# A planned one-core kernel (gated linear attention, then a two-layer MLP): a planner that follows both DMA streams in time, the first attention blocks in the first layer's PSUM banks, and decay factors taken straight from PSUM

## The chip, the cores and the metric

One core of one Trainium2 chip. The metric is the device time of one execution in microseconds, as the median of three runs; the profile shows one more execution, with its own time.

## The reference

```python
def _attn_ref(q, k, v, f_logit):            # (4, 8, 768, 48) each
    f = 1.0 / (1.0 + np.exp(-f_logit))
    for t in range(S):
        state = f[:, :, t, :, None] * state + np.einsum('bhd,bhe->bhde', k[:, :, t], v[:, :, t])
        y[:, :, t] = np.einsum('bhd,bhde->bhe', q[:, :, t], state)

def _moe_ref(x, w_in, w_out):               # x (3072, 384), w_in (384, 2048), w_out (2048, 384)
    h = x @ w_in
    g = 0.5 * (h + np.sqrt(h * h + 4.0))
    return g @ w_out
```

The tokens of all heads of a batch are laid side by side, so that the output of the attention is the input of the MLP.

## The kernel before, in words

The 3072 tokens are 24 blocks of 128 (six to a batch, so that the state starts anew at blocks 0, 6, 12 and 18), and two blocks are a **pair**, p = 0 to 11. A pair goes through these steps:

- **Loads.** SP issues eight DMAs per pair (f, q, k, v for two blocks, 192 KB each, in runs of 192 bytes). The weights, eight pieces of `w_in` and eight of `w_out`, are issued on POOL and cast to fp16 on the way.
- **Logs** (`add_logs`): ScalarE takes exp and log of f into `ls`; POOL or VectorE splits `ls` into two fp16 parts, `lhi` and `llo`.
- **Decays** (`add_decays`): TensorE sums the logs down the block into a bank `hps`, in whose last columns two half-block sums per head stand as well. ScalarE makes `ea` and `eap` of it by exp; POOL or VectorE multiplies them into q and k (`qk`); v is cast to fp16; VectorE copies the half-block sums to `nls`. In `add_gammas` VectorE adds neighbouring sums into `gi`, ScalarE takes the exp, and VectorE spreads it over `gam`, the decay of the state from block to block.
- **Attention** of a block (`add_attention`, `add_state`): transposes of `qk` (on TensorE for pairs 0 to 4, by DMA for 5 to 11), scores `sc`, masked `pm`, the state update `u` and `sn`, the output `y`, its transpose into `xT`.
- **First layer** (`add_mlp1`): four steps per pair. A step is 12 matmuls into two banks `hps`, two squares `hsq` and one root `r` on ScalarE, two gates `g` on VectorE, which free the banks. There are five banks `hps` (NH), which the decays use too, two banks "a" (NA) for the attention, and one bank `o` (NO).
- **Second layer** (`add_mlp2`): per block 16 matmuls into `o` in four quarters; quarter n needs gates of step n and pieces 2n and 2n+1 of `w_out`; then a copy to `o_sb` and a store, issued by POOL or SP.

ScalarE needs one table for exp and log and another for the root, so the logs and decays are gathered in seven stretches (`GROUPS`): in stretch g the decays of group g and the logs of group g+1.

The order is not written by hand. A `Plan` takes every step with a duration, what it waits for and which buffers it takes; it simulates the engines and, among steps that can start at about the same time, takes the one with the lowest due time. The due times are the tables `BASE` (by part and pair) and `SHIFT` (by kind of step), and `ENG` says which engine takes a step that two could take. What comes out is one fixed order on each engine, in which every engine runs in order. Loads had one queue, in the order of `ORDER`, and a pass over both streams (`flows`) gave the DMAs their landing times for the next pass.

Of the kernel before, what the change touches and what calls it, by code (L numbers as in the profile page):

```python
# [63 lines left out]

class Op:
    __slots__ = ("eng", "dur", "deps", "emit", "due", "allocs", "uses", "end", "kind", "dma", "ins", "flow", "issued")

    def __init__(self, eng, dur, emit, deps=(), due=0.0, allocs=(), uses=(), kind=None, dma=None, ins=()):
# [22 lines left out]
class Plan:  # L91
# [39 lines left out]
    def flows(self):  # L131


        todo = {"SP": [], "POOL": []}
        for op in self.order:
            if not isinstance(op, str) and op.dma is not None:
                todo[op.eng].append([op.issued, op.dma[0], op])
        t = 0.0
        while todo["SP"] or todo["POOL"]:
            live = {e: q[0] for e, q in todo.items() if q and q[0][0] <= t + 1e-9}  # L140
            later = [q[0][0] for e, q in todo.items() if q and e not in live]
            if not live:
                t = min(later)
                continue
            rate = {"SP": 0.35, "POOL": 0.65} if len(live) == 2 else {e: 1.0 for e in live}
            step = min([x[1] / rate[e] for e, x in live.items()] + [a - t for a in later])
            t += step
            for e, x in live.items():
                x[1] -= step * rate[e]
                if x[1] <= 1e-9:  # L150
                    x[2].flow = t + x[2].dma[1] - x[2].issued
                    todo[e].pop(0)

    def run(self, passes=3):
        for n in range(passes):
            for ops in self.queues.values():
                for op in ops:
                    op.end = None
                    for b in op.uses + op.allocs:
                        b.ring.bufs = []  # L160
# [723 lines left out]
```

## Time and profile before

| | before |
|---|---|
| median of 3 runs | 222.13 us (222.03 to 222.53) |
| profiled execution | 222.69 us, of which the span of the trace is 220.9 us |
| busy in the span | TensorE 183.0, ScalarE 170.3, VectorE 156.7, POOL 86.0 us |
| DMA | 32.09 MB, 61.8% of the 16 engines' span on SP's queue, 13.2% on POOL's |

What lies outside of the span is 1.8 us. The ends of TensorE's matmuls are modelled, so that neighbours overlap: its busy time is more than the time that it takes from one start to the next.

### The profile page before, as it was taken

What the parts mean: (1) busy time and instruction counts of PE and PEld (TensorE: products, weight loads), DVE (VectorE), ACT (ScalarE), POOL (GpSimd) and SP (SyncE); (2) the same over time, 40 slices, a digit from 0 to 9 for tenths busy, and PEclk for the clock granted to TensorE, in tenths of its full rate; (3) what the DMA queues carried; (4) which work ended last, traced back from release to release, by engine and by line L of the source; (5) the groups of instructions that cost most, each with busy time, mean ns of one, the idle gap of its engine ahead of it and who ended that gap; (6) DMA issues with size and microseconds to landing.
All of it is one profiled execution on the core that took longest, in us unless ns stands there. A gap on an engine that the chain in (4) does not pass through costs nothing.

```text
span 220.9 us, 4812 instructions
## 1 busy us (share of the span) xinstructions
PE 183.0 (83%) x1870; PEld 132.6 (60%) x1870; DVE 156.7 (71%) x285; ACT 170.3 (77%) x262; POOL 86.0 (39%) x95
## 2 busy tenths in 40 slices
PE   0445837928999999789988998799999999999973
PEld 0223624715777576567666776476677777777641
DVE  5056716836976989998998988998879888663220
ACT  5306339469899999779999999599979999986710
POOL 8959379531014408440993118703900000000010
PEclk9999987995999999999999999999999999999998
DMA  7999999999999999499999999741572302111101
GB/s 135 164 178 168 196 182 201 220 179 214 215 200 239 227 213 187 110 221 154 233 177 184 171 223 186 136 106 53 81 153 47 74 18 58 53 39 37 71 36 71
DMA packets 128262, 32.09 MB, mean 145 GB/s; under 512 B 121088, under 2 KB 127616, under 8 KB 128240
## 3 DMA queue, kind: packets, MB, share of 16 engines
q1 hardware_dynamic: 122032, 26.09, 61.8%
q0 software_dynamic: 6208, 5.70, 13.2%
q8 instruction: 14, 0.23, 0.4%
q14 instruction: 8, 0.07, 0.1%
HBM read 25.17 MB, written 4.72 MB: 135 GB/s over the span
## 4 chain that ended last, share of the span: by engine, by line
PE 54%; ACT 12%; DVE 11%; DMA 10%; SPq 8%; issue 3%; POOL 1%; ACTq 0%; DVEq 0%; POOLq 0%
PE o L788 23%; PE hps L748 21%; SPq L371 8%; DMA ld_v<-in_v_dram 5%; DMA ld_f<-in_f_logit_dram 4%; DVE qk L495 3%; ACT r L763 3%; PE sc L626 2%; ACT hsq L754 2%; DVE gam L555 2%; PE tr L601 1%; ACT ls L438 1%; ACT L851 1%; PE y L649 1%; DMA xT<-y 1%
## 5 line engine op out<-in xcount | busy, mean ns | idle before, releaser
L788 PE MATMUL o<-w_out,g 128*128 128x384 f16 x384 | 73.2, 326 | 2.9 <-DVE o_sb L799 1.4
L771 DVE SCALAR_TENSOR_TENSOR g<-hps,r 128x512 f16<-128x512 f32 x96 | 61.7, 685 | 18.9 <-ACT r L763 18.1
L748 PE MATMUL hps<-xT,w_in 128*128 128x256 f16 x576 | 73.6, 279 | 1.1 <-DMA xT<-y 0.8
L748 PEld LDWEIGHTS <-w_in 128*128 128x128 f16 x576 | 56.1, 100 | 12.9 <-DMA xT<-y 1.2
L754 ACT ACTIVATE hsq<-hps 128x512 f16<-128x512 f32 x96 | 54.5, 592 | 6.9 <-PE hps L748 5.4
L763 ACT ACTIVATE r<-hsq 128x1024 f16<-128x1024 f16 x48 | 50.7, 1057 | 1.4
L788 PEld LDWEIGHTS <-g 128*128 128x128 f16 x384 | 35.3, 97 | 22.6 <-issue 4.0
L803 POOL DMA_DIRECT2D out_dram<-o_sb x13 | 7.3, 563 | 72.4 <-DVE o_sb L799 41.4
L633 DVE TENSOR_TENSOR pm<-sc,mask 128x512 f16<-128x512 f32 x48 | 31.0, 682 | 4.6 <-PE sc L626 4.6
L433 ACT ACTIVATE ld_f<-ld_f 128x768 f32<-128x768 f32 (+1 forms) x14 | 10.7, 763 | 18.2 <-DMA ld_f<-in_f_logit_dram 18.2
L495 POOL TENSOR_TENSOR qk<-ld_q,ea 128x768 f16<-128x768 f32 (+1 forms) x10 | 14.8, 1483 | 19.0 <-ACT ea L489 16.6
L502 POOL CAST v<-ld_v 128x768 f16<-128x768 f32 (+1 forms) x11 | 8.6, 779 | 27.7 <-DMA ld_v<-in_v_dram 27.7
L444 POOL TENSOR_TENSOR llo<-ls,lhi 128x768 f16<-128x768 f32 (+1 forms) x12 | 17.3, 1449 | 3.4 <-DVE lhi L441 2.8
L626 PE MATMUL sc<-qkT 48*128 48x128 f16 x192 | 11.3, 230 | 6.7 <-ACT qkT L605 3.3
L495 POOL TENSOR_TENSOR qk<-ld_k,eap 128x768 f16<-128x768 f32 (+1 forms) x10 | 15.2, 1518 | 0.0
L601 PE MATMUL tr<-ident,qk 128*128 128x128 f16 x80 | 8.7, 267 | 7.7 <-POOL qk L495 5.7
L489 ACT ACTIVATE ea<-hps 128x384 f32<-128x384 f32 x24 | 10.8, 502 | 5.5 <-PE hps L482 5.4
L475 PE MATMUL hps<-lhi,wcent 128*128 128x384 f16 x24 | 8.5, 352 | 7.5 <-POOL lhi L441 7.5
L626 PEld LDWEIGHTS <-qkT 48*128 48x128 f16 x192 | 6.3, 99 | 12.9 <-issue 7.8
L649 PEld LDWEIGHTS <-pm 128*128 128x128 f16 x192 | 10.2, 99 | 4.0 <-issue 2.6
L797 ACT COPY o_sb<-o 128x384 f32<-128x384 f32 x10 | 4.8, 477 | 9.6 <-PE o L788 9.6
L601 PEld LDWEIGHTS <-qk 128*128 128x128 f16 x80 | 6.5, 118 | 9.4 <-POOL qk L495 6.8
(56 smaller groups left out, 237.7 us busy)
## 6 DMA issues: line engine op xcount, KB each, us to landing
ld_f<-in_f_logit_dram SPq DMA_DIRECT2D x24, 192.0 KB, 4.1
ld_q<-in_q_dram SPq DMA_DIRECT2D x24, 192.0 KB, 4.0
ld_k<-in_k_dram SPq DMA_DIRECT2D x24, 192.0 KB, 4.0
ld_v<-in_v_dram SPq DMA_DIRECT2D x24, 192.0 KB, 4.6
out_dram<-o_sb POOLq DMA_DIRECT2D x13, 192.0 KB, 3.3
out_dram<-o_sb SPq DMA_DIRECT2D x11, 192.0 KB, 2.1
w_in<-in_moe_w_in_dram POOLq DMA_DIRECT2D x8, 192.0 KB, 7.0
w_out<-in_moe_w_out_dram POOLq DMA_DIRECT2D x8, 192.0 KB, 5.9
```

The source lines that it names most:

```text
L371: (nc.gpsimd if cast else nc.sync).dma_start(out=T["v16" if cast else name, p][:, r], in_=src_of[name][b][:, c * C:(c + 1) * C, :].rearran ...
L444: eng_of[lg[p, x].eng].tensor_tensor(out=llo[p % NL][:, x:y, :, 0:D], in0=T["ls", p][:, x:y], in1=lhi[p % NL][:, x:y, :, 0:D], op=ALU.subt ...
L495: eng_of[mu[p, x, i].eng].tensor_tensor(out=qk[p % NB][:, x:y, i, :, 0:D], in0=T[name, p][:, x:y], in1=T[e, p][:, x:y], op=ALU.mult)
L601: nc.tensor.transpose(out=tr[:, s * NP + j, :], in_=qk[p % NB][:, i, s, 2 * j:2 * j + 2, :], identity=ident16)
L626: nc.tensor.matmul(out=T["sc", r, s][:, j, :], lhsT=qkT[o:o + D, NP + j, :], rhs=qkT[o:o + D, j, :], start=True, stop=True)
L633: nc.vector.tensor_tensor(out=T["pm", r][:, s], in0=T["sc", r, s], in1=mask16.unsqueeze(1).broadcast_to([128, NP, C]), op=ALU.mult)
L649: nc.tensor.matmul(out=y[:, j, s], lhsT=T["pm", r][:, s, j, :], rhs=T["v16", p][:, i, 2 * j + s, :], start=(c == 0), stop=(c == 0 or s == 1))
L748: nc.tensor.matmul(out=hb[:, a, :], lhsT=w_in16[j2][:, j, a * 128:(a + 1) * 128], rhs=T["xT", p][:, j, :], start=(j == 0), stop=(j == NJ - 1))
L754: nc.scalar.activation(out=T["hsq", p, j4][:, a], in_=T["h", p, j2], func=AF.Square, scale=1.0)
L763: nc.scalar.activation(out=T["r16", p, j4], in_=T["hsq", p, j4], func=AF.Sqrt, scale=0.25, bias=1.0)
L771: nc.vector.scalar_tensor_tensor(out=T["g", p][:, jn:jn + 2, :].rearrange("p a t -> p (a t)"), in0=T["h", p, 2 * j4 + a], scalar=0.5, in1= ...
L788: nc.tensor.matmul(out=T["o", p, i], lhsT=T["g", p][:, jn, i * C:(i + 1) * C], rhs=w_out16[jn // 2][:, jn % 2, :], start=(jn == 0), stop=( ...
```

## The change

- **The planner** carries both DMA streams along with the engines, in time order (`transfer`): a DMA lands when its stream has moved it, with SP at 0.4 and POOL at 0.65 of the rate while both have work. It lets SP issue only while there is room in its queue (`room`), keeps VectorE's `hi`, `lo`, `qk`, `v16` and `wcast` and POOL's work apart in time, and has new durations.
- **Loads** of f, q, k and v have queues of their own with due times (`"L"` in `BASE`), so that their order is free. Pair 2 is loaded and multiplied by the block, too (`FINE`).
- **Weights.** The first piece of each matrix is loaded on SP as fp32 (`wst`) and cast on VectorE. The other 14 still go by POOL, but now behind the v cast of pair 2 (`AFTER`), and in the plan no more than four are under way (`OUTSTANDING`).
- **q and k** of `qk` have engines of their own, and the product of k does not wait for that of q.
- **Banks.** The attention of blocks 0 to 3 takes banks of `hps` instead of the two banks "a" (`EARLY`).
- **Decay factors.** VectorE copies one half-block sum to `nls` and adds the other from PSUM into `gi`; ScalarE's exp writes `gam` itself, in two halves of 64 partitions. The rest of `gam` is set to zero once. The two VectorE steps of `add_gammas` are gone.
- All tables have new numbers.

```diff
-XBAR = [5, 6, 7, 8, 9, 10, 11]
+XBAR = [5, 6, 7, 8, 9, 10, 11, 13, 14, 15, 16, 17, 18, 19, 21, 22, 23, 24, 25, 26, 27]
...
-FINE = [0, 1]
+FINE = [0, 1, 2]
+
+AFTER = {'in': 2, 'out': 2}
+
+OUTSTANDING = 4
...
+EARLY = 4
...
+    RATE = {"SP": 0.4, "POOL": 0.65}
+    ROOM = 2048
...
+    def transfer(self, streams, t, until):
+
+        while t < until - 1e-9:
+            live = [e for e, q in streams.items() if q and q[0][0] <= t + 1e-9]
+            later = [q[0][0] for e, q in streams.items() if q and e not in live]
+            rate = {e: self.RATE[e] if len(live) == 2 else 1.0 for e in live}
+            step = min([streams[e][0][1] / rate[e] for e in live] + [x - t for x in later] + [until - t])
             t += step
...
+                            if eng == "SP" and op.dma is not None:
+                                t = max(t, self.room(op))
+                            elif eng == "POOL":
+                                t = max(t, locked)
+                            elif eng == "DVE" and op.kin in self.PORT:
+                                t = max(t, free.get("POOL", 0.0))
...
+        w_ready[which, i] = []
+        n = i + (8 if which == "out" else 0)
+        for inline in (NPAIR + n in XBAR,):
+            if inline:
+                def direct():
+                    nc.gpsimd.dma_start(out=dst, in_=src)
+
+                op = P.add("p" + which, "POOL", 0.75, direct, due=1.0 * i, dma=(1.3, 384))
+                direct_ops.append(op)
...
-                    nc.vector.tensor_copy(out=nls[b % 2][:, c + r], in_=nl)
+                    if c + r < NC - 1:
+                        nc.vector.tensor_copy(out=nls[b % 2][:, c + r], in_=nl[:, :, 1])
+                    if c + r > 0:
+                        nc.vector.tensor_tensor(out=gi[b % 2][:, c + r - 1], in0=nl[:, :, 0], in1=nls[b % 2][:, c + r - 1], op=ALU.add)
...
+            def ex(b=b, c0=c0, c1=c1):
+                for s in range(2):
+                    nc.scalar.activation(out=gam[b % 2][64 * s:64 * s + 64, c0:c1, :, s], in_=gi[b % 2][64 * s:64 * s + 64, c0:c1],
+                                         func=AF.Exp, scale=-1.0)
...
+    def bank(r):
+
+        return Buf(ring("h", NH) if r < EARLY else ring("a", NA))
...
+    for a, op in zip(direct_ops, direct_ops[OUTSTANDING:]):
+        op.deps.append(a)
+    for op in direct_ops:
+        if AFTER[op.kin[1:]] is not None:
+            op.deps.append(dec[AFTER[op.kin[1:]], PR - 1][1])
```

What this does to the order shows at three places. First, POOL from its last memset on. Before, four pieces of `w_in` stand ahead of its first `lhi`:

```order
L336 MEMSET qk3_113 128x32x16
L396 DMA w_in16_0_94<-in_moe_w_in_dram 128x3x256
L396 DMA w_in16_1_95<-in_moe_w_in_dram 128x3x256
L396 DMA w_in16_2_96<-in_moe_w_in_dram 128x3x256
L396 DMA w_in16_3_97<-in_moe_w_in_dram 128x3x256
L441 CAST lhi0_114<-ls_152 128x8x48
L444 TENSOR_TENSOR llo0_118<-ls_152,lhi0_114 128x8x48
```

Now the first piece on POOL stands behind the casts of v of pair 2 (`v16_335`), and `w_out` from its third piece on behind the `lhi` of pair 3 (`lhi3`):

```order
L448 CAST lhi2_114<-ls_315 128x8x48
L509 CAST v16_335<-ld_v_283 128x384
L404 DMA w_in16_1_93<-in_moe_w_in_dram 128x3x256
...
L451 TENSOR_TENSOR llo2_118<-ls_315,lhi2_114 128x8x48 x2
...
L404 DMA w_in16_7_99<-in_moe_w_in_dram 128x3x256
L502 TENSOR_TENSOR qk2_110<-ld_k_333,eap_501 128x8x48
L502 TENSOR_TENSOR qk2_110<-ld_q_312,ea_499 128x8x48
L404 DMA w_out16_1_101<-in_moe_w_out_dram 128x2x384
L448 CAST lhi3_115<-ls_533 128x16x48
L404 DMA w_out16_2_102<-in_moe_w_out_dram 128x2x384
```

So eight pieces can be issued before `lhi3`, and the other six wait for it. Second, the first DMAs of SP, before (`ld_f_138` to `ld_v_159` are pair 0, the next four pair 1, `ld_f_313` pair 2):

```order
L371 DMA ld_f_138<-in_f_logit_dram 128x8x48 x2
L371 DMA ld_q_141<-in_q_dram 128x8x48 x2
L371 DMA ld_k_144<-in_k_dram 128x8x48 x2
L371 DMA ld_v_159<-in_v_dram 128x8x48 x2
L371 DMA ld_f_191<-in_f_logit_dram 128x8x48 x2
...
L371 DMA ld_f_313<-in_f_logit_dram 128x8x48 x2
```

and now (`ld_f_142` is pair 0, `ld_f_147` pair 1; the fifth f of SP's order is that of pair 3, behind `ld_k_333` of pair 2):

```order
L413 DMA wst_140<-in_moe_w_out_dram 128x2x384
L376 DMA ld_f_142<-in_f_logit_dram 128x8x48
L413 DMA wst_144<-in_moe_w_in_dram 128x3x256
L376 DMA ld_f_142<-in_f_logit_dram 128x8x48
L376 DMA ld_f_147<-in_f_logit_dram 128x8x48 x2
L376 DMA ld_v_155<-in_v_dram 128x8x48 x2
...
L376 DMA ld_f_254<-in_f_logit_dram 128x8x48 x2
L376 DMA ld_v_283<-in_v_dram 128x8x48 x2
L376 DMA ld_q_312<-in_q_dram 128x8x48 x2
L376 DMA ld_k_333<-in_k_dram 128x8x48 x2
```

The two blocks' loads of pairs 0 and 1 are now grouped by kind, f and v ahead of q and k. Third, ScalarE where the first layer begins. Before, the log of f of pair 2 is followed by two steps of the first layer, and the decays of pair 2 come after them, in a stretch of their own:

```order
L438 ACTIVATE ls_413<-ld_f_313 128x768
L551 ACTIVATE gi_354<-gi_354 128x8
L754 ACTIVATE hsq_437<-hps_392 128x512
L754 ACTIVATE hsq_437<-hps_393 128x512
L851 ACT_TABLE_LOAD
L763 ACTIVATE r16_460<-hsq_437 128x1024
...
L849 ACT_TABLE_LOAD
L489 ACTIVATE ea_546<-hps_510 128x384
```

Now the decays of pair 2 (`ea_499`) and the exp and log of f of pair 3 (`ld_f_374`) stand ahead of the first square:

```order
L660 CAST y16_414<-y_415 128x384
L496 ACTIVATE ea_499<-hps_442 128x384
L496 ACTIVATE eap_501<-hps_442 128x384
...
L440 ACTIVATE ld_f_374<-ld_f_374 128x768
L445 ACTIVATE ls_533<-ld_f_374 128x768
L555 ACTIVATE gam0_120<-gi0_124 64x8 x2
L758 ACTIVATE hsq_560<-hps_535 128x512
```

Seven steps of the first layer then follow with no exps or logs between them; before, the stretch stands behind the first two.

## Rows read from the trace of the kernel before

**Rows 1.** The page's busy line of the core.

```profile
PE 183.0 (83%) x1870; PEld 132.6 (60%) x1870; DVE 156.7 (71%) x285; ACT 170.3 (77%) x262; POOL 86.0 (39%) x95
```

**Rows 2.** Windows: stretch, its length, busy us (instructions) per engine, granted clock, DMA, GB/s.

```profile
0.00:53.50 53.50, 27.46 (x284) 19.46 (x284) 26.20 (x58) 27.45 (x46) 35.63 (x51) 0.93 1.08 182
80.00:160.00 80.00, 73.32 (x846) 53.04 (x845) 72.19 (x129) 72.54 (x117) 40.49 (x31) 1.00 0.84 162
160.00:200.00 40.00, 40.00 (x389) 30.61 (x388) 32.29 (x54) 36.13 (x53) 1.61 (x3) 1.00 0.26 61
```

**Rows 3.** Timeline of ScalarE: start, us, instruction, idle before and what ended it.

```profile
3.59 0.52 ACT L433 ACTIVATE ld_f<-ld_f 128x384 f32<-128x384 f32 x1 [1.57 <-DMA ld_f<-in_f_logit_dram]
16.84 0.52 ACT L433 ACTIVATE ld_f<-ld_f 128x384 f32<-128x384 f32 x1 [5.29 <-DMA ld_f<-in_f_logit_dram]
31.20 0.84 ACT L433 ACTIVATE ld_f<-ld_f 128x768 f32<-128x768 f32 x1 [6.29 <-DMA ld_f<-in_f_logit_dram]
46.05 0.84 ACT L433 ACTIVATE ld_f<-ld_f 128x768 f32<-128x768 f32 x1 [4.62 <-DMA ld_f<-in_f_logit_dram]
48.19 1.09 ACT L754 ACTIVATE hsq<-hps 128x512 f16<-128x512 f32 x2
```

**Rows 4.** Timeline of SP: two issues of f, with nothing but loads between them.

```profile
50.16 1.83 SPq L371 DMA_DIRECT2D ld_f<-in_f_logit_dram  x2
57.61 1.57 SPq L371 DMA_DIRECT2D ld_f<-in_f_logit_dram  x2
```

**Rows 5.** Timeline of POOL: three issues of weights.

```profile
3.72 3.23 POOL L396 DMA_DIRECT2D w_in<-in_moe_w_in_dram  x4
32.02 2.19 POOL L396 DMA_DIRECT2D w_out<-in_moe_w_out_dram  x3
36.71 2.16 POOL L396 DMA_DIRECT2D w_out<-in_moe_w_out_dram  x3
```

**Rows 6.** Timeline of ScalarE: a stretch of exps and logs begins and ends; a root.

```profile
65.08 1.28 ACT L849 ACT_TABLE_LOAD   x1
71.35 1.06 ACT L754 ACTIVATE hsq<-hps 128x512 f16<-128x512 f32 x2
114.94 1.06 ACT L763 ACTIVATE r<-hsq 128x1024 f16<-128x1024 f16 x1
```

**Rows 7.** The chain that ended last: start, us, what.

```profile
70.79 0.89 PE tr L601 x16
...
76.17 1.31 PE hps L748 x12
77.48 0.65 PE o L788 x4
```

**Rows 8.** Groups of VectorE by line: tile, shape, count | busy us, mean ns | idle before.

```profile
L633 DVE TENSOR_TENSOR pm<-sc,mask 128x512 f16<-128x512 f32 x48 | 31.0, 682 | 4.6 <-PE sc L626 4.6
...
L555 DVE TENSOR_TENSOR gam<-gi,half 128x8 f32<-128x8 f32 (+3 forms) x9 | 7.8, 861 | 4.6 <-ACT gi L551 4.6
L495 DVE TENSOR_TENSOR qk<-ld_q,ea 128x768 f16<-128x768 f32 x4 | 6.4, 1612 | 0.1
L546 DVE TENSOR_TENSOR gi<-nls 128x4 f32<-128x4 f32 (+3 forms) x9 | 5.0, 552 | 0.2
L502 DVE CAST v<-ld_v 128x768 f16<-128x768 f32 x3 | 2.5, 838 | 1.7 <-DMA ld_v<-in_v_dram 1.7
```

**Rows 9.** Timelines of VectorE and POOL: gi and qk beside POOL and alone.

```profile
11.78 1.02 DVE L546 TENSOR_TENSOR gi<-nls 128x4 f32<-128x4 f32 x1
11.78 0.99 POOL L495 TENSOR_TENSOR qk<-ld_q,ea 128x384 f16<-128x384 f32 x1
67.28 0.96 DVE L495 TENSOR_TENSOR qk<-ld_q,ea 128x768 f16<-128x768 f32 x1
68.42 0.16 DVE L546 TENSOR_TENSOR gi<-nls 128x4 f32<-128x4 f32 x1
```

**Rows 10.** Timeline of ScalarE: the exp of gi and what it waited for.

```profile
141.52 0.20 ACT L551 ACTIVATE gi<-gi 128x4 f32<-128x4 f32 x1 [2.50 <-DVE gi L546]
```

More of the change, by code (lines that the diff above doesn't have):

```diff
@@ L107, in add @@
         op = Op(eng, dur, emit, due=due, **kw)
+        op.kin = queue
         self.queues.setdefault((eng, queue), []).append(op)
@@ L129, in ready @@
         return t
[L131 to L146, printed above, removed]
+    def transfer(self, streams, t, until):
[4 more added lines that the diff above has]
+            step = min([streams[e][0][1] / rate[e] for e in live] + [x - t for x in later] + [until - t])
@@ L147, in flows @@
             t += step
-            for e, x in live.items():
+            for e in live:
+                x = streams[e][0]
                 x[1] -= step * rate[e]
                 if x[1] <= 1e-9:
[L151 to L160, printed above, removed]
-            self.order = []
-            self.once()
-            if n + 1 < passes:
-                self.flows()
@@ L166, in once, with room, run @@
-    def once(self):
+                    x[2].done = t
+                    x[2].end = t + self.LAG + (self.CROWD if len(live) == 2 else 0.0)
+                    streams[e].pop(0)
+        return until
+    def room(self, op):
+        n = op.dma[1]
+        for x in reversed(self.sent):
+            n += x.dma[1]
+            if n > self.ROOM:
+                return x.done - op.dur
+        return 0.0
+    def run(self):
         heads = {k: 0 for k in self.queues}
         free = dict(START)
-        dma_free = 0.0
-        served = []
+        streams, clock, self.sent, locked = {"SP": [], "POOL": []}, 0.0, [], 0.0
@@ L331 @@
     gam = [konst.tile([128, NC, NP, 2], FP32, name=f"gam{i}") for i in range(2)]
-    nls = [konst.tile([128, NC, NP, 2], FP32, name=f"nls{i}") for i in range(2)]
+    nls = [konst.tile([128, NC, NP], FP32, name=f"nls{i}") for i in range(2)]
+    gi = [konst.tile([128, NC, NP], FP32, name=f"gi{i}") for i in range(2)]
+    for t in gam:
+        nc.vector.memset(t, 0.0)
     for t in lhi + llo:
@@ L613, in add_attention @@
             add_state(r - 1, p, due + 1.0)
-        sc_b = [Buf(ring("a", NA)) for _ in range(2)]
+        sc_b = [bank(r) for _ in range(2)]
         def sc():
@@ L805, in add_mlp2 @@
             oo = oc_op[p, i] = P.add("ev", None, {"DVE": 0.555, "ACT": 0.49}, oc, at=p * PR + i, deps=[last], p=p, due=due, allocs=[os_b], uses=[o_b])
-            st_op[p, i] = P.add("out", None, {"SP": 0.5, "POOL": 0.85}, st, at=p * PR + i, deps=[oo], p=p, due=due, uses=[os_b], dma=(0.6, 1.8))
-    for what in ORDER.split():
-        if what[0] == "P":
-            for n in "fqkv":
-                add_load(int(what[1:]), n)
-        elif what[0] in "io":
-            for i in range(int(what[1]), int(what[2]) + 1):
-                add_weight("in" if what[0] == "i" else "out", i)
-        else:
-            for n in what[:-1]:
-                add_load(int(what[-1]), n)
+            st_op[p, i] = P.add("out", None, {"SP": 0.5, "POOL": 0.6}, st, at=p * PR + i, deps=[oo], p=p, due=due, uses=[os_b], dma=(0.6, 128))
     for p in range(NPAIR):
         for n in "fqkv":
-            if (n, p, 0) not in ld:
-                add_load(p, n)
+            add_load(p, n)
+    for which in ("in", "out"):
+        for i in range(8):
+            add_weight(which, i)
     NG = len(GROUPS)
@@ L839 @@
         add_mlp2(p)
-    if WDMA:
-        for (which, i), op in w_ready.items():
-            if AFTER[which] is not None:
-                op.deps.append(dec[AFTER[which], PR - 1][1])
+    for a, op in zip(direct_ops, direct_ops[OUTSTANDING:]):
[3 more added lines that the diff above has]
+            op.deps.append(dec[AFTER[op.kin[1:]], PR - 1][1])
     P.run()
```

184 lines of the change are left out of this document (80 added, 104 removed), and 15 rows, old and new, of tables (BASE, SHIFT).

## The prediction, as it was put on record before the kernel ran

> **What bounds the kernel now.** I read the page first. TensorE is busy 83% of the span and ScalarE 77% [rows 1], so neither alone explains it. The windows then split the span in three. From 160 to 200 us TensorE is busy all 40 us; from 80 to 160 it is idle 6.7 us (80 less 73.3) while VectorE is idle only 7.8; and in the first 53.5 us TensorE and ScalarE are busy about half the time, with the DMA share above 1 [rows 2]. So the kernel is bound by DMA at the front, by TensorE at the end, and by a tight chain of three engines in the middle. The chain of waits agrees: loads and SP's queue to about 50 us, TensorE from there on.
>
> What does the front wait for? On the timeline ScalarE sits 6.3 us until f of pair 2 lands at 31.20 and 4.6 us until f of pair 3 lands at 46.05 [rows 3]. TensorE's granted clock is 0.93 of its upper level over this stretch, and 1.00 in the two later ones [rows 2]. The end is full, so the front is where time can be won: whatever lets TensorE and ScalarE run without a break sooner moves the end, less the work that they still owe.
>
> **The front, step by step.** *Price of a DMA.* With loads alone SP issues the eight of a pair in 57.61 − 50.16 = 7.45 us, 0.93 us each [rows 4]. A piece of weights costs what is missing: from 3.59 to 16.84 eight loads land (7.45 us) beside four pieces of `w_in` issued from 3.72 on, which leaves 5.8 us, 1.45 each; from 31.20 to 46.05 another eight and the six pieces of `w_out` that are issued by 38.87, which leaves 7.4 us, 1.23 each [rows 3, 5]. I take 1.28, nearer to the later one, which has no start of a stream in it.
>
> *When f of pair 3 lands.* Before, at 46.05, behind 24 loads and about 14 pieces. Now ahead of it or with it are 26 loads (three pairs, and its own two), two staged pieces, and of POOL's pieces at most eight, since the ninth stands behind `lhi3`, which needs this f. The first load took to 3.59, so the stream begins about 3.59 − 0.93 = 2.66. Then 2.66 + 26 × 0.93 = 26.8; two staged pieces, whose fp32 write the trace doesn't show, between a load's 0.93 and twice a piece (2.56): I take 1.3 each, nearest to a piece, since they read the same bytes: 29.4. With six pieces of POOL's ahead 37.1, with all eight 39.7. The plan's limit of four is no wait in the kernel (the order shows `w_in` 5 to 7 with none), so I take nearly all: **39.0**. Bounds: four pieces and cheap staging, 33.8; eight and dear staging, 42.2.
>
> *Is that the last input?* The loads of pairs 0 and 1 are in by 2.66 + 16 × 0.93 + 2.6 = 20.1 (q and k of pair 0 come later than before, their f at about the same time). Four blocks of attention follow, whose eight masks alone take VectorE 5.5 us [rows 8]; with about as much again for products, copies and states, an estimate from that row, `xT` of pair 0 is there by about 32, and `llo2` on POOL stands behind the v of pair 2 (24 us) and four issues of 0.8 us [rows 5]: near 28. `w_in` lands by about 40 us, since all of it is ahead of or with that f, and the fourth step, which needs the last piece, comes at 47. So f of pair 3 is last.
>
> *ScalarE.* Before, from 46.05 to the square at 48.19 took 2.1 us [rows 3]: the first square now at 41.0. Seven steps of two squares, 1.06, and a root, 1.06, with one table load of 1.28 are 16.0 us: 57.0. The next stretch took 71.35 − 65.08 = 6.3 us [rows 6]: at 63.3 ScalarE is where it was at 71.35, but with seven steps done instead of eight, 2.1 us. **Its lead is 5.9 us.**
>
> *TensorE* at these two moments owes more now: one step of the first layer (1.31), two quarters of the second (2 × 0.65) and two transposed blocks (0.89) [rows 7], 3.5 us. **Its lead is 71.35 − 63.3 − 3.5 = 4.5 us.** Between 4.5 and 5.9, I take **4.8**: TensorE ends the kernel, but its 6.7 us of idle time to 160 us come where ScalarE's stretches leave it without work, and quarters still owed fill them.
>
> **Decay factors.** Nine `gi` and nine `gam` on VectorE go (12.8 us busy [rows 8]); of the small copies `nls` 20 of 24 stay, and 20 adds from PSUM come. What was on the path is ScalarE's wait for `gi` of 2.5 us, with its table load and root behind it [rows 10]; the exp is now one instruction more of 0.2 us, nine times, beside some 50 us of ScalarE's idle time over the span [rows 1]. Between 0 and 2.5 I take **1.5**, since VectorE, which was late there, is as full as before (next).
>
> The adds' price shows nowhere. An old `gi` started with a POOL product at 11.78 and took 1.02 us, one alone took 0.16 [rows 9]; all nine took 0.55 on average [rows 8]. I take 0.16, since it now reads one of its two inputs from PSUM, as `nls` did; 0.55 is the other bound. The Trainium skill (SBUF — State Buffer, Who interferes with whom) says that a VectorE instruction with two SBUF inputs contends with a GpSimd instruction that reads SBUF and that the later of the two fully blocks, and one with a single SBUF input does not. The two rows agree with its first half; by its second half the adds take 3.2 us in all, by the old mean 11.
>
> **VectorE's added work.** It takes over three v casts of 768 columns and two halves, three `llo`, net two `lhi`, seven halves of `qk`, two weight casts and one output copy. At the price of a `qk` alone, 0.96 for 768 columns [rows 9], three `llo` and seven halves of `qk` are 6.2 us; casts and copies at half of it, some ten, 4.8; adds 3.2: 14.2, less 12.8, **+1.4 us**. At the means with POOL in the way (v 0.84, `qk` 1.61 [rows 8], an add 0.55) `llo` and halves are 10.5, casts and copies 8.4, adds 11: 29.9 less 12.8, +17. Much of it lies in the first 53.5 us, where VectorE is idle 27. From 80 to 160, where it is idle 7.8, I charge **0.5**, near the lower end because POOL is busy only half of that stretch [rows 2]; bounds 0 and 8.5, half of the +17. The same section of the skill speaks against this part: fp32 casts from SBUF to SBUF also hold the shared ports in its two-port modes, so that POOL's next instruction waits them out. By that rule the far bound, not the near one, holds where casts and POOL meet.
>
> **The tail** keeps its 48 matmuls of the second layer behind the last step, but the last two blocks' `y` are now copied by ScalarE two steps before their pair begins, and a transposing DMA lies between. I charge **0.5**, between 0 and 1.5. `EARLY` I cost at nothing: its banks are free until the first layer starts, and if attention holds them late, f of pair 3 at 39 covers it by some 7 us.
>
> **The sum.** 4.8 + 1.5 − 0.5 − 0.5 = 5.3 us. The profiled execution took 222.69 us, a span of 220.9 and 1.8 outside; its span becomes 215.6 and its time 217.4. The median before is 0.56 below that execution: **216.8 us**.
>
> **The rivals.**
> 1. *The middle loosens too.* If TensorE's idle 6.7 us from 80 to 160 halve, because more quarters are owed and no `gi` is waited for, 3.4 us more go: 213.4. For it: the end is full, so any idle time removed counts. Against: the same count of stretches is left, five, with two table loads each.
> 2. *The lead is given back in the middle*, and the change does not do what it says: VectorE, 72 of 80 us busy, meets each group's decays with more work ahead of the gates, and gates late by half a microsecond in each of nine groups undo 5 us: 221.8. For it: VectorE takes over 11 us of other work at 90% busy. Against: with the adds cheap, its sum stays.
> 3. *VectorE becomes the bound, and the kernel is slower.* Place: the `qk`, `llo` and v casts of pairs 3 to 9 on VectorE, ahead of the gates that free the banks `hps`. If they run at the means with POOL in the way, 8.5 us come after 53.5 us: 216.8 + 8.0 = 224.8. It decides from 5.8 us of such time on the path. For it: `qk` on VectorE has taken 1.61 on average and 0.96 at best. Against: the new plan keeps these steps and POOL's apart, and POOL has fewer of them.
>
> **How the numbers follow.** The forecast, 214.5 to 220: 0.55. Rival 1 and anything faster: 0.15. Rival 2, 220 to 222.6: 0.13, of which 0.06 is above 221.7. Rival 3 and what is slower: 0.17. A measurement of this kernel tells some 0.2% (0.45 us) from no change: faster 0.55 + 0.15 + 0.07 = 0.77, same 0.06, slower 0.17. The front's bounds move the sum by +5 (f at 33.8, where `xT` would come last, so hardly more than 4) and −3.2 (42.2); with rival 1 below and the near part of rival 3 above, 8 in 10 lie in 212.0 to 223.5. The forecast's own range is 214.5 to 220.
>
> **What would show it.** Right: ScalarE's exp of f of pair 3 near 39 us and the first square near 41; then seven steps with under 2 us of idle time; the square behind the decays of pair 3 at about 63; no wait for `gi`; adds near 0.16 us; TensorE full from 160 us to its last quarter. Wrong: f of pair 3 after 43, or a first square that waits for `xT` or a bank long after it; v of pair 3, which VectorE casts ahead of the first gate, later than 43; or VectorE's `qk` and casts at 1.3 us and more with ScalarE idle behind banks that are not free.

## The result, and the profile after

The changed kernel takes **216.28 us** (median of 4 runs, 214.53 to 217.09), 0.9704 of the kernel before (95% interval 0.9627 to 0.9782): 216.8 was forecast. The profiled execution took 216.77 us, a span of 215.0. The first rows are the page's busy times and, under "...", the windows that answer to [rows 2] (busy time of TensorE, its weight loads, VectorE, ScalarE and POOL, then the granted clock, the DMA share and GB/s).

```profile
PE 183.1 (85%) x1870; PEld 132.1 (61%) x1870; DVE 158.2 (74%) x303; ACT 168.1 (78%) x270; POOL 71.5 (33%) x83
...
0.00:53.50 53.50, 30.39 (x301) 21.26 (x302) 30.02 (x70) 27.58 (x50) 29.80 (x48) 0.94 1.28 189
80.00:160.00 80.00, 76.62 (x842) 55.60 (x840) 71.54 (x134) 74.39 (x122) 29.00 (x22) 1.00 0.98 167
160.00:200.00 40.00, 39.86 (x392) 29.90 (x391) 28.72 (x51) 34.77 (x53) 6.60 (x6) 1.00 0.34 72
```

TensorE does 2.9 us more work in the front, is idle 3.4 us instead of 6.7 from 80 to 160, and is full at the end. ScalarE's timeline answers to [rows 3, 6]:

```profile
37.75 0.84 ACT L440 ACTIVATE ld_f<-ld_f 128x768 f32<-128x768 f32 x1 [3.88 <-DMA ld_f<-in_f_logit_dram]
38.62 0.84 ACT L445 ACTIVATE ls<-ld_f 128x768 f32<-128x768 f32 x1
39.37 0.41 ACT L555 ACTIVATE gam<-gi 64x8 f32<-64x8 f32 x2
39.81 1.08 ACT L758 ACTIVATE hsq<-hps 128x512 f16<-128x512 f32 x2
40.91 1.28 ACT L848 ACT_TABLE_LOAD   x1
...
59.97 1.28 ACT L846 ACT_TABLE_LOAD   x1
...
66.13 0.58 ACT L758 ACTIVATE hsq<-hps 128x512 f16<-128x512 f32 x1
```

f of pair 3 comes at 37.75 (39.0 forecast, 46.05 before) and the first square at 39.81 (41.0). But the seven steps end at 59.97, not 57.0, and the square behind the decays of pair 3 comes at 66.13, not 63.3. By the prediction's own sum ScalarE's lead is 71.35 − 66.13 − 2.1 = 3.1 us and TensorE's 5.2 − 3.5 = 1.7, against the 5.9 and 4.5 forecast.

POOL's issues of weights until f of pair 3 is there answer to [rows 5]; the last line is the time from issue to landing of the pieces of `w_in` (least, median and most):

```profile
26.87 3.25 POOL L404 DMA_DIRECT2D w_in<-in_moe_w_in_dram  x4
31.87 2.32 POOL L404 DMA_DIRECT2D w_in<-in_moe_w_in_dram  x3
36.11 0.76 POOL L404 DMA_DIRECT2D w_out<-in_moe_w_out_dram  x1
...
DMA to landing us min/median/max: 5.1/6.6/8.2
```

What held the squares up stands on VectorE, and behind it on TensorE:

```profile
43.62 0.65 DVE L509 CAST v<-ld_v 128x768 f16<-128x768 f32 x1 [4.76 <-DMA ld_v<-in_v_dram]
44.19 0.94 DVE L451 TENSOR_TENSOR llo<-ls,lhi 128x768 f16<-128x768 f32 x1
45.05 1.27 DVE L775 SCALAR_TENSOR_TENSOR g<-hps,r 128x512 f16<-128x512 f32 x2
...
45.78 2.72 PE L752 MATMUL hps<-xT,w_in 128*128 128x256 f16 x12 [5.72 <-DVE g L775]
48.29 1.49 PE L792 MATMUL o<-w_out,g 128*128 128x384 f16 x4
```

The cast of v of pair 3 waits 4.76 us for its load, and the first gate (whose root was done at 43.3) stands behind it. TensorE has no free bank until then: it sits 5.7 us, and its next step takes 2.72 us, not 1.31 [rows 7]. So the front gave less than forecast, and yet the total came out. The rest lies behind that square. The same view, cut from it to the end, for before and then for after:

```profile
71.35:220.90 149.55, 137.85 (x1414) 99.67 (x1411) 116.25 (x201) 126.10 (x193) 46.90 (x40) 1.00 0.60 123
```

```profile
66.13:215.00 148.87, 140.11 (x1439) 101.34 (x1436) 117.04 (x215) 128.18 (x203) 39.97 (x33) 1.00 0.74 133
```

TensorE is idle 149.55 − 137.85 = 11.7 us there before, and 8.8 after, with more work to do. The added and removed steps of the decay factors, as the view by tile groups them (minimum, median and maximum in ns), answer to [rows 8, 9]:

```profile
L518 DVE TENSOR_TENSOR gi<-hps,nls x20: 146/151/163, 12.1 to 161.0; 128x4 f32<-128x4 f32 x20
L555 ACT ACTIVATE gam<-gi x18: 189/203/221, 13.5 to 161.4; 64x4 f32<-64x4 f32 x6, 64x8 f32<-64x8 f32 x6, 64x16 f32<-64x16 f32 x4, 64x12 f32<-64x12 f32 x2
```

### The profile page after: what moved, and what is told of

Read it like the earlier page. It is cut to its first block, busy times and chain, and to the rows that moved or that the text cites. A ratio compares the mean times of both kernels' runs of the same rounds, so it can differ in the third digit from the quotient of the medians.

```text
span 215.0 us, 4826 instructions
## 1 busy us (share of the span) xinstructions
PE 183.1 (85%) x1870; PEld 132.1 (61%) x1870; DVE 158.2 (74%) x303; ACT 168.1 (78%) x270; POOL 71.5 (33%) x83
## 4 chain that ended last, share of the span: by engine, by line
PE 43%; ACT 24%; DMA 14%; SPq 10%; issue 4%; DVE 3%; ACTq 0%; DVEq 0%
PE o L792 19%; PE hps L752 18%; SPq L376 10%; ACT r L767 7%; ACT hsq L758 7%; DMA xT<-y 6%; DMA ld_v<-in_v_dram 5%; DMA ld_f<-in_f_logit_dram 2%; ACT ld_f L440 2%; DMA ld_q<-in_q_dram 2%; PE sc L630 2%; ACT ls L445 1%; DVE g L775 1%; ACT L848 1%; ACT ea L496 1%
## 5 line engine op out<-in xcount | busy, mean ns | idle before, releaser
L758 ACT ACTIVATE hsq<-hps 128x512 f16<-128x512 f32 x96 | 53.8, 591 | 12.3 <-PE hps L752 11.3
L502 POOL TENSOR_TENSOR qk<-ld_q,ea 128x768 f16<-128x768 f32 (+1 forms) x8 | 13.2, 1648 | 19.9 <-ACT ea L496 16.5
L451 POOL TENSOR_TENSOR llo<-ls,lhi 128x384 f16<-128x384 f32 (+1 forms) x10 | 13.3, 1335 | 1.8 <-DVE lhi L448 1.4
L502 POOL TENSOR_TENSOR qk<-ld_k,eap 128x768 f16<-128x768 f32 (+1 forms) x7 | 10.9, 1552 | 7.3 <-ACT eap L496 5.4
L662 DVE CAST y<-y 128x384 f16<-128x384 f32 x17 | 9.4, 552 | 4.7 <-PE y L653 4.5
L653 PE MATMUL y<-v,pm 128*128 128x48 f16 x192 | 12.4, 189 | 0.5 <-DVE pm L637 0.4
L803 DVE COPY o_sb<-o 128x384 f32<-128x384 f32 x15 | 8.3, 555 | 5.0 <-PE o L792 4.9
L722 DVE TENSOR_TENSOR sn<-u,gam 128x384 f16<-128x384 f32 x20 | 11.0, 549 | 1.2 <-ACT gam L555 0.6
L483 PE MATMUL hps<-llo,wcent 128*128 128x384 f16 x24 | 8.8, 366 | 3.1 <-POOL llo L451 3.1
L445 ACT ACTIVATE ls<-ld_f 128x768 f32<-128x768 f32 (+1 forms) x15 | 10.7, 715 | 0.8
```

The lines of the kernel that those rows point to most:

```text
L451: eng_of[lg[p, x].eng].tensor_tensor(out=llo[p % NL][:, x:y, :, 0:D], in0=T["ls", p][:, x:y], in1=lhi[p % NL][:, x:y, :, 0:D], op=ALU.subt ...
L502: eng_of[mu[p, x, i].eng].tensor_tensor(out=qk[p % NB][:, x:y, i, :, 0:D], in0=T[name, p][:, x:y], in1=T[e, p][:, x:y], op=ALU.mult)
L653: nc.tensor.matmul(out=y[:, j, s], lhsT=T["pm", r][:, s, j, :], rhs=T["v16", p][:, i, 2 * j + s, :], start=(c == 0), stop=(c == 0 or s == 1))
L758: nc.scalar.activation(out=T["hsq", p, j4][:, a], in_=T["h", p, j2], func=AF.Square, scale=1.0)
```

## The experiments

**Theory:** the time comes from the front, since POOL's pieces of weights no longer stand ahead of f of pair 3, and the front gave less than forecast because the cast of v of pair 3 holds up the gates. **Rival:** the front is worth little, and the middle gives the time. After the first group a third theory joined these, the *layout theory*, below.

All traces side by side: the time against before (ratio, 95% interval), the exp of f of pair 3, the square behind the decays of pair 3, what is left from there to the end, and how long SP took to issue eight loads that run alone (for the two rows of the kernel before, from the start of the first issue to that of the ninth, some 0.4 us between issues included; for the others the issues' own times).

| kernel | ratio | f of pair 3 | square | to the end | eight loads |
|---|---|---|---|---|---|
| before | 1 | 46.05 | 71.35 | 149.55 | 7.45 |
| after | 0.9704 (0.9627–0.9782) | 37.75 | 66.13 | 148.87 | 8.35 |
| after, again | 0.9697 (0.9652–0.9743) | 39.60 | 66.14 | 147.46 | 8.33 |
| after, weights ahead | 0.9996 (0.9954–1.0037) | 48.25 | 74.26 | 147.94 | 8.28 |
| after, old decay factors | 0.9698 (0.9656–0.9739) | 36.28 | 62.57 | 151.03 | 7.14 |
| after, v behind gates | 0.9562 (0.9510–0.9614) | 37.23 | 62.47 | 147.33 | 8.39 |
| after + 32 bytes | 0.9534 (0.9501–0.9567) | 36.94 | 63.85 | 146.65 | 7.08 |
| after + 64 bytes | 0.9680 (0.9634–0.9726) | 38.25 | 66.20 | 147.00 | 7.98 |
| after, v, + 32 bytes | 0.9528 (0.9489–0.9566) | 35.46 | 62.22 | 148.38 | 6.96 |
| the same, squares first | 0.9436 (0.9392–0.9480) | 35.93 | 60.01 | 147.79 | 7.28 |
| before + 32 bytes | 1.0059 (1.0015–1.0103) | 45.86 | 71.41 | 149.49 | 7.99 |
| before, new decay factors | 0.9846 (0.9799–0.9893) | 46.09 | 73.16 | 146.14 | – |
| before, late w_out | 0.9922 (0.9876–0.9968) | 42.44 | 69.11 | 149.19 | – |

The edits on the order are made behind the plan, on its finished list, so that all else keeps its place (a new plan would move everything): `move` takes steps out of the list and puts them before or behind another.

**The changed kernel once more,** as a mark: no edit.

> The changed kernel once more, as the mark for the other runs of this group. Both theories: 216.3 us, between 214.5 and 217.1 as its four runs so far; its front as before in its trace: exp of f of pair 3 at 37.8, first square at 39.8, square behind the decays of pair 3 at 66.1.

215.69 us. As expected; f of pair 3 came 1.8 us later than in the first trace, and the square not at all, since v was there no later (43.86).

**Weights ahead.**

```diff
     P.run()
+    move(direct_ops[0:4], before=hi[0, 0])
+    move(direct_ops[4:7], before=hi[2, 0])
+    move(direct_ops[7:14], behind=lg[2, 1])
```

> The changed kernel, but GpSimd issues its 14 pieces of weights where the kernel before did: w_in 1 to 4 ahead of the first lhi, w_in 5 to 7 ahead of lhi of pair 2, w_out 1 to 7 behind llo of pair 2, all ahead of lhi of pair 3. Front theory (the time won is that f of pair 3 lands ahead of most of w_out, so that the next stretch starts sooner): f of pair 3 has six pieces more ahead of it, 6 x 1.28 = 7.7 us, so its exp comes at 44 to 46, the first square at 46 to 48, the square behind the decays of pair 3 at 70 to 73, and the time is 219 to 222. Rival, middle theory (the front is worth little, since gates and banks hold it back anyway; the time comes from the later stretches): the exp may be late, but the time is 216.3 to 217.5.

222.96 us, and by the ratio nothing is left of the gain. In the traced execution (224.03 us, one of the slower of ten) POOL issues `w_out` from 33.83 on, and f lands at 48.25, even later than expected:

```profile
33.83 5.05 POOL L404 DMA_DIRECT2D w_out<-in_moe_w_out_dram  x7
...
48.25 0.84 ACT L440 ACTIVATE ld_f<-ld_f 128x768 f32<-128x768 f32 x1 [11.55 <-DMA ld_f<-in_f_logit_dram]
```

From the square to the end it needs 147.9 us, as the changed kernel does: the 8.1 us by which the square is late come out at the end nearly whole (7.3 between the medians, 6.6 by the ratios). Front theory, and its rival falls.

**Old decay factors in the new order.**

```diff
-    nls = [konst.tile([128, NC, NP], FP32, name=f"nls{i}") for i in range(2)]
-    gi = [konst.tile([128, NC, NP], FP32, name=f"gi{i}") for i in range(2)]
+    nls = [konst.tile([128, NC, NP, 2], FP32, name=f"nls{i}") for i in range(2)]
+    half32 = konst.tile([128, 2], FP32, name="half32")
...
+                    nc.vector.tensor_copy(out=nls[b % 2][:, c + r], in_=nl)
...
+    for o3, d, a, z in old:          # a, z: sums and spread of before; o3: the exp
+        last = max(d, key=P.order.index)
+        P.order.insert(P.order.index(last) + 1, a)
...
+        P.order.insert(at, z)        # at: the first step that the plan starts 0.22 us behind the exp
```

> The changed kernel with the decay factors of the kernel before: both sums copied from PSUM, added in SBUF by VectorE, exp, spread by VectorE, put in where these inputs are there by the plan; the rest of the order is as in the changed kernel. Front theory: the decay factors are worth 0 to 2.5, 1.5 at the likeliest, so 216.3 to 218.8, at the likeliest 217.8, with waits of ScalarE for gi of some 0.3 to 2.5 in a stretch. Rival, middle theory: most of the 6 us is in this path, and 4 us go: 219.5 to 221.

215.69 us: no difference, at first sight. But the trace says that two things cancel. The square comes 3.6 us sooner, and the stretch behind it is 3.6 us longer, TensorE being idle 10.75 us in it instead of 7.5. The second is the old path. VectorE's steps with both inputs in SBUF, and TensorE's waits behind them:

```profile
L557 DVE TENSOR_TENSOR gi<-nls x9: 152/434/2364, 11.9 to 159.1; 128x4 f32<-128x4 f32 x3, 128x8 f32<-128x8 f32 x3, 128x16 f32<-128x16 f32 x2, 128x12 f32<-128x12 f32 x1
...
PE u L729 <- DVE pm L651: 1.6, 1, 1.6
PE u L729 <- DVE xT L712: 1.2, 1, 1.2
```

The first is for the most part not the decay factors' doing: every load is faster. For the changed kernel, and then for this one, SP's issues:

```profile
10.18 4.12 SPq L376 DMA_DIRECT2D ld_q<-in_q_dram  x4
14.34 4.23 SPq L376 DMA_DIRECT2D ld_k<-in_k_dram  x4
```

```profile
9.94 3.65 SPq L377 DMA_DIRECT2D ld_q<-in_q_dram  x4
13.63 3.49 SPq L377 DMA_DIRECT2D ld_k<-in_k_dram  x4
```

Eight loads in 7.14 us instead of 8.35. A smaller part seems to be an effect of the old factors after all, since with the new ones and fast loads the square comes at 63.85 (below): VectorE spreads `gam` ahead of its copy of `qkT`, the scores come later, and TensorE's wait in front of the gates falls into two:

```profile
39.84 0.28 PE L644 MATMUL sc<-qkT 48*128 48x128 f16 x1 [2.53 <-DVE qkT L623]
...
43.61 2.72 PE L766 MATMUL hps<-xT,w_in 128*128 128x256 f16 x12 [1.85 <-DVE g L789]
```

The table shows the pattern: 7.45 in before and 7.14 here, 8.3 to 8.4 in all others of this group. Before and this run have `half32`, a tile of 8 bytes that takes 32 in each partition; without it the buffers of f begin at 84,640 (those of q, k and v whole multiples of 3,072 behind), 32 bytes past a multiple of 64, and with it at 84,672 (in before at 75,456), which are multiples. That is the **layout theory**, and the second group tests it. (The tile moves all that stands behind it, not the loads' buffers alone. In this run it stands behind the weights' buffers, which keep the changed kernel's place: the loads are fast without them.)

**v of pair 3 behind the gates.**

```diff
     P.run()
+    move([dec[3, 0][1]], behind=g_ops[0][1])     # v16 of pair 3, behind the first four gates
```

> The changed kernel, but VectorE casts v of pair 3 behind the first four gates instead of ahead of them. Front theory (the lead was 1.7 to 3.1 instead of 4.8 because this cast waited for its load until 43.6 and held up the gates, and so the banks and TensorE, until 45.1): first gate at 43.3 to 43.6, first layer's matmuls at 44.1 instead of 45.8, square behind the decays of pair 3 at 64 to 65 instead of 66.1, and 1 to 2 us less: 214.3 to 215.3. Rival (the lead doesn't carry to the end, which the middle sets): the gates come sooner and the time stays within 0.4 of the changed kernel's, 215.9 to 216.7.

213.42 us; the traced execution, of 211.64, is the fastest of six. First gate and step three, VectorE and then TensorE:

```profile
42.78 1.29 DVE L775 SCALAR_TENSOR_TENSOR g<-hps,r 128x512 f16<-128x512 f32 x2 [1.95 <-ACT r L767]
...
43.52 2.72 PE L752 MATMUL hps<-xT,w_in 128*128 128x256 f16 x12 [2.85 <-DVE g L775]
46.03 1.02 PE L792 MATMUL o<-w_out,g 128*128 128x384 f16 x4
46.89 1.47 PE L752 MATMUL hps<-xT,w_in 128*128 128x256 f16 x12
```

The gate now waits for its root, the square comes 3.7 us sooner, at 62.47, and the time falls by 1.4% (0.9697 to 0.9562): the cast was what held the gates, and the lead carries. It is larger than expected. Two things in the trace go with that, neither run by itself: f came 0.5 us sooner than in the changed kernel's first trace, and the fourth step runs at the upper level of the clock again (1.47 us, below).

**32 bytes more.**

```diff
     nc.vector.memset(hvec[64:128, 1:2], 1.0)
+    pad = konst.tile([128, 8], FP32, name="pad")
+    nc.vector.memset(pad, 0.0)
```

> The changed kernel with 32 bytes more in each partition of SBUF ahead of the weights' and loads' buffers (one small tile that nothing reads). In the changed kernel these buffers begin 32 bytes past a multiple of 64, since half32 is gone; in the kernel before, and in the run with the old decay factors for the loads, they begin at a multiple of 64. Layout theory (a load of 192-byte runs takes 1.02 to 1.04 us at the one place and 0.88 to 0.92 at the other, and this slowed the front): eight loads in 7.0 to 7.5 us, exp of f of pair 3 at 34.5 to 36.5, square behind the decays of pair 3 at 61.5 to 63.5, and 212 to 213.5 us. Rival (the loads' rate is chance of an execution, or comes from the old decay factors): loads at 1.02 and more, and 215.7.

0.9559 (0.9521 to 0.9597), five executions between 212.40 and 214.09; the profiled one took 456.49 us, and nothing is read from it. So it was run again:

> The changed kernel with 32 bytes more in each partition once more, for a trace of an ordinary execution (the last one took twice the time). Layout theory: eight loads in 7.0 to 7.5 us, exp of f of pair 3 at 34.5 to 36.5, square behind the decays of pair 3 at 61.5 to 63.5, 0.954 to 0.958 of before. Rival: 0.968 to 0.972.

212.40 us, 0.9534, and the loads are as fast as expected:

```profile
10.29 3.49 SPq L378 DMA_DIRECT2D ld_q<-in_q_dram  x4
13.82 3.59 SPq L378 DMA_DIRECT2D ld_k<-in_k_dram  x4
```

f came at 36.94 and the square at 63.85, each 0.4 later than the expected end; the cast of v waits until 41.83 and TensorE 5.1 us for the gates, as in the changed kernel, but two microseconds sooner.

**64 bytes more** (`[128, 16]` instead of `[128, 8]`).

> The changed kernel with 64 bytes more in each partition instead of 32, so that its buffers again begin 32 bytes past a multiple of 64. Layout theory: eight loads in 8.1 to 8.4 us, and the time of the changed kernel, 0.968 to 0.972 of before. Rival (any shift helps, or the added memset does): loads at 0.88 to 0.92 each, and 0.954 to 0.958.

215.16 us, 0.9680: the time of the changed kernel. SP's issues:

```profile
10.72 3.76 SPq L378 DMA_DIRECT2D ld_q<-in_q_dram  x4
14.53 4.22 SPq L378 DMA_DIRECT2D ld_k<-in_k_dram  x4
```

7.98 us, a little less than expected, but not 7.1. It is not the shift or the added memset, it is where the buffers begin. In the same group 32 bytes more are worth 215.16 − 212.40 = 2.8 us.

**32 bytes more in the kernel before.** The same `pad`.

> The kernel before, with the same 32 bytes, which move its buffers off the multiple of 64. Layout theory: eight loads in 8.1 to 8.3 us instead of 7.45, exp of f of pair 3 at 48 to 49.5 instead of 46.05, and 224 to 226 us. Rival (no effect of the layout): 222.2 and loads at 0.93.

224.95 us, 0.6% more. The sign is right and the size half of what was expected: eight loads alone take 7.99 us, but f of pair 3 lands no later (45.86). The traced execution, of 222.65 us, is the fastest of twelve and no longer than the one traced of the kernel before, so it can't show where the price falls; that stays open.

**New decay factors alone,** in the order of before.

```diff
-                    nc.vector.tensor_copy(out=nls[b % 2][:, c + r], in_=nl)
+                    if c + r < NC - 1:
+                        nc.vector.tensor_copy(out=nls[b % 2][:, c + r], in_=nl[:, :, 1])
+                    if c + r > 0:
+                        nc.vector.tensor_tensor(out=gi[b % 2][:, c + r - 1], in0=nl[:, :, 0], in1=nls[b % 2][:, c + r - 1], op=ALU.add)
...
-            o1 = P.add("gam", "DVE", 0.2, sums, deps=d, p=p, due=0.5, allocs=[gi_b])
+            o1 = P.add("gam", "DVE", 0.2, none, deps=d, p=p, due=0.5, allocs=[gi_b])
...
-            o3 = P.add("gam", "DVE", 0.2, spread, deps=[o2], p=p, due=0.5, uses=[gi_b])
+            o3 = P.add("gam", "DVE", 0.2, none, deps=[o2], p=p, due=0.5, uses=[gi_b])
```

> The kernel before with the new decay factors alone (copy of one sum, add from PSUM, two exps into gam; the two steps that fall away leave their places empty), in the order and the layout of before. Theory of the prediction: 0 to 2.5 us less, 1.5 at the likeliest, 219.7 to 222.2, with the wait of ScalarE for gi gone. Rival from the run with the old factors in the new order (TensorE idle behind that square 10.8 us instead of 7.5): 3 us less, 219 to 219.5. Rival: they are worth nothing, since TensorE's owed work fills the wait: 222.2.

220.10 us, 1.5% (3.4 us) less. From the square to the end:

```profile
73.16:219.30 146.14, 136.96 (x1408) 99.22 (x1406) 109.75 (x201) 126.93 (x197) 47.10 (x40) 1.00 0.59 124
```

146.1 us instead of 149.6: 3.4 us shorter, of which 2.5 is idle time of TensorE and 0.9 busy time (its rows hold six matmuls fewer). By the time and by this stretch it is what the first rival said, and more than the prediction's bound. (In this execution, one of 221.07 us, the square itself came 1.8 us later, though f did not; why, was not traced.)

**Late w_out alone,** in the order of before.

```diff
     P.run()
+    move([w_ready["out", i] for i in range(4, 8)], behind=lg[3, 0])
```

> The kernel before, but GpSimd issues w_out 4 to 7 behind llo of pair 3 instead of ahead of lhi of pair 3: one part of the change alone, in the old order, the old decay factors and the old layout. Front theory: f of pair 3 has four pieces less ahead of it, 4 x 1.23 = 4.9 us, so its exp comes at 41 to 42 instead of 46.05, the square behind the decays of pair 3 at 66 to 68 instead of 71.35, and the time is 3 to 5 us less, 217.5 to 219.5. Rival: the first layer's gates or the quarter that needs w_out 4 wait as long, since these pieces now land at 47 to 52 us: 221 to 223.

220.62 us, 0.8% (1.7 us) less, between the two. f comes 3.6 us sooner, the square 2.2. Part of the rest is what the rival said: the quarters wait 1.3 us for `w_out`, which was 0.2 before. VectorE's cast of v waits for its load as well, but no longer than before, where it waited 1.72 at 53.10. VectorE's timeline, and TensorE's waits from 30 to 72 us:

```profile
48.60 0.72 DVE L502 CAST v<-ld_v 128x768 f16<-128x768 f32 x1 [1.28 <-DMA ld_v<-in_v_dram]
...
PE o L788 <- DMA w_out<-in_moe_w_out_dram: 1.3, 2, 0.7
```

In the old order half of f's 3.6 us reaches the end; in the new one, by the run with the weights ahead, f is 8.7 to 10.5 us later and the time 6.6 to 7.3, two thirds or more.

**v behind the gates and 32 bytes.** Both edits.

> Both: v of pair 3 cast behind the first four gates, and the 32 bytes. Layout theory with the front theory: the loads are faster, so v is there sooner and the cast costs less where it stood; f of pair 3 at 34.5 to 36, square behind the decays of pair 3 at 60 to 61.5, and 210 to 212 us. Rival (loads of v or xT bind once f is sooner): no better than the better of the two alone, 212 to 213.5.

212.50 us, 0.9528: no better than 32 bytes alone, the number that the rival gave. Its cause, a load of v or `xT`, did not hold the first gate, which waits for its root (1.95 us). f comes 1.8 us sooner than with v alone, and the square 0.25: TensorE has done its two steps sooner, sits 5.0 us instead of 2.85 for the first gate, and then works at the lower level of its clock for longer. Its windows behind that wait, with v alone and with both:

```profile
43.50:47.00 3.50, 3.48 (x18) 2.36 (x18) 3.33 (x6) 2.56 (x5) 0.58 (x1) 0.58 1.29 199
47.00:50.00 3.00, 3.00 (x41) 2.69 (x39) 2.66 (x6) 2.97 (x5) 0.00 (x0) 1.00 1.28 185
```

```profile
41.70:47.90 6.20, 6.15 (x28) 3.99 (x28) 5.30 (x10) 4.15 (x6) 0.62 (x1) 0.51 1.28 196
```

Against 32 bytes alone the square is 1.6 us sooner, and the stretch behind it 1.7 us longer. There `xT` does bind: TensorE's waits for it from 62 us on, with 32 bytes alone and with both:

```profile
PE hps L754 <- DMA xT<-y: 0.4, 1, 0.4
```

```profile
PE hps L754 <- DMA xT<-y: 2.1, 2, 1.6
```

Why the transposing DMA is later there was not run.

**Squares first.** On top of both, the first step's squares go ahead of the exp of f of pair 3, where ScalarE waits for its load.

```diff
+    ln = hi[3, 0].deps[0]
+    move([ln.deps[0], ln], behind=squares[1])    # exp and log of f of pair 3, behind the first two squares
```

> The changed kernel with v of pair 3 cast behind the first four gates, the 32 bytes, and the first step's two squares (and the exp of the decay factors) ahead of the exp of f of pair 3 on ScalarE, which waits there for its load anyway. Front theory: root 1 starts 1.5 us sooner behind f of pair 3 (its load stays at 35 to 36), the first gate at 39.3 to 40 instead of 41.0, TensorE's idle time ahead of the third step 3.5 instead of 5.0, the square behind the decays of pair 3 at 60 to 61.2 instead of 62.2, and 1 to 1.5 us less than that kernel without the squares: 0.946 to 0.949 of before. Rival (what the front gives is lost to TensorE's lower clock behind an idle time of any such length): 0.952 to 0.955 of before.

**209.92 us, 0.9436: faster than both kernels.**

```profile
33.46 0.60 ACT L760 ACTIVATE hsq<-hps 128x512 f16<-128x512 f32 x1 [0.34 <-PE hps L754]
34.45 0.60 ACT L760 ACTIVATE hsq<-hps 128x512 f16<-128x512 f32 x1 [0.40 <-PE hps L754]
35.93 0.84 ACT L442 ACTIVATE ld_f<-ld_f 128x768 f32<-128x768 f32 x1 [0.88 <-DMA ld_f<-in_f_logit_dram]
...
38.96 1.06 ACT L769 ACTIVATE r<-hsq 128x1024 f16<-128x1024 f16 x1
...
40.80 1.82 PE L754 MATMUL hps<-xT,w_in 128*128 128x256 f16 x12 [3.41 <-DVE g L777]
```

The root starts 3.0 us behind f's landing instead of 4.5, TensorE waits 3.4 us instead of 5.0, and the square comes at 60.01, 2.2 us sooner: what ate the sooner f was the wait in front of the gates, with the lower clock behind it.

## Why the prediction was right, point by point

The time was right, and the sum behind it was not: two terms were too small, and a loss was missed that made up for them. What was right is the mechanism of the front; that the total came within 0.5 us (216.28 against 216.8) is luck.

- **f of pair 3 at 39.0:** right as a landing (37.75, and 38.25 to 39.60 in two further executions with this layout). Its price of a load, 0.93 from [rows 4], was wrong here: loads took 8.35 / 8 = 1.04. That alone would make 26 loads 2.9 us later. What can make up for it is POOL's pieces, of which nearly all eight were taken to be ahead. By the rows of POOL above some four of them had landed by 37.75, an estimate: the last four were issued from 31.87 on, and none of `w_in` took less than 5.1 us.
- **"Is that the last input?"** f is, for the squares. For the gates it is v of pair 3, at 43.62: the case that the prediction named as the one that would make it wrong, and there it did so.
- **The front, +4.8.** Measured in the changed kernel: 1.7 to 3.1. With loads as fast as the prediction took them the square comes at 63.85 (32 bytes more) or 62.57 (old decay factors, TensorE's wait in two), which by the same sum is a lead of 5.4 or 6.7 for ScalarE and 4.0 or 5.3 for TensorE. So the lead was about right, and the layout took 2.3 to 3.6 us of it back. Too large was what the sum took off for work still owed: of 8.05 us by which the square comes sooner, 3.25 there and 1.0 for VectorE and the tail. In the run with the old factors the square comes 8.8 us sooner, and the stretch behind it is only 1.5 us longer, all in all: TensorE is busy 2.4 us more there, not 3.5, and idle 0.95 less (10.75 against 11.7). Order and weights so gave 6.7 us where the sum had 3.8. That the front is where the time is won is shown by the weights put ahead again: 0.9996. The new order of the loads, the two staged pieces and `EARLY` were not taken out one by one; they are in the 6.7.
- **The missed loss, about 3 us.** The prediction has no term for `half32`, the tile that goes. What that does to where all later tiles begin was not looked at. 0.9697 without and 0.9534 to 0.9559 with 32 bytes: 3.1 to 3.6 us.
- **Decay factors, +1.5, bounds 0 to 2.5:** too small. 3.4 us in the old order; in the new one, with loads alike, 0.9698 against 0.9534 to 0.9559, again 3.1 to 3.6 (though the weights' buffers, `qk`, `lhi` and `llo` too differ by 32 bytes in place between these two). The term priced only ScalarE's wait for `gi` [rows 10]. In the changed kernel ScalarE waits for no `gi`, as foretold; but in the run with the old factors it waits 0.9 us only, and the loss stands in VectorE's steps: up to 2.36 us for a sum over 12 columns, with masks, copies and TensorE behind them.
- **The adds at 0.16:** right, 0.151 at the median and 0.163 at most, of 20. The Trainium skill (SBUF — State Buffer, Who interferes with whom) says that a VectorE instruction with at most one SBUF input, outside its two-port modes, does not contend with GpSimd, and that one with two does when GpSimd reads SBUF. The row agrees, and so does the old sum with two, at 0.15 to 2.36.
- **VectorE's added work, −0.5:** no run takes it out alone. In the run with the old factors, which has all of that work, the stretch behind the square is 1.5 us longer than before's, with TensorE busy for 2.4 us more. So it can't have cost much; its size stays open.
- **The tail, −0.5:** TensorE is idle 0.14 us from 160 to 200. Its price was not run by itself.
- **The rivals.** TensorE's idle time from 80 to 160 did halve, by the 3.3 us that rival 1 gave. It named two causes, more quarters owed and no wait for `gi`, and the runs do not part them: in that window TensorE is idle 3.7 us with the old factors in the new order, and 4.1 with the new factors in the old one, so that either alone gives most of it. Over the whole stretch behind the square the old factors cost it 10.75 us, against 8.8 and 7.5 in the changed kernel. Rivals 2 and 3 did not come: VectorE's `qk` of 768 columns runs at 0.95 to 1.28 us on average behind 60 us, and TensorE waits 0.3 us in all for gates behind 66.

By the runs: order and weights −6.7 (old factors, fast loads), decay factors −3.4, layout +3.1, in all −7.0, where −6.5 was measured (215.69 against 222.17); the decay factors' part is taken from the old order. Forecast were −3.8, −1.5 and nothing.

## What to carry to other kernels

A small tile that is taken away moves every tile behind it: look where the buffers of the DMAs begin, before and after. When a load comes sooner, look for the load after it, and for what stands behind the instruction that waits for it. And a total that comes out as forecast proves no term of it: put back one part at a time, and where nothing changes, look in the trace for two changes that cancel.

## What the runs showed of the hardware

- **Where a load's buffer begins.** DMAs of 192-byte runs, 192 KB each, took 0.87 to 0.93 us, on the mean of eight, into buffers that begin at a multiple of 64 bytes and 1.00 to 1.05 at 32 bytes past one, in eleven traces without an exception. The shift of all tiles was worth 2.8 to 3.6 us of 222 in this order, 1.3 in the old one. Whether 64 or a smaller share of a larger unit is what counts, no run tells. The Trainium skill (DMA: Bandwidth & Descriptors, How a descriptor splits into AXI transactions) says that a transaction that reads begins at a multiple of 256 bytes, and that bytes ahead of the start cost beats of 32 bytes. If writes into SBUF went the same way, which the Trainium skill doesn't say there, runs of 192 bytes would take 9 beats on average at a multiple of 64 and 10 at 32 past it, an estimate from that rule: 11% more. The rows show 7% in the old order (7.45 and 7.99) and 10 to 21% between any two traces of the new one.
- **TensorE's clock behind a wait.** After 5.0 us without matmuls (both edits) the granted clock was 0.51 for the next 6.2 us, the lower of its two levels, 1.2 GHz; after 5.1 (32 bytes alone) 0.51 over 5.1; after 2.85 us (v alone) it was 0.58 over 3.5 us, and 1.00, 2.4 GHz, from 47.0 on; after 3.4 us (squares first) 0.67 over 5.2, and then 1.00. So the same wait costs twice: in the run with both edits only 0.25 of the 1.8 us by which f was sooner was left at the square.
